# VectorE's 256 low-part columns of an attention block read from the score bank in PSUM, and one tile a block turned by TensorE in all four batches

## Chip, cores and metric

The kernel runs on one core of a Trainium2 chip. The metric is the device time of one execution in microseconds (us). Lower is better. The engines are TensorE (PE; its weight loads are listed apart, as PEld), VectorE (DVE), ScalarE (ACT), GpSimd (POOL) and SyncE (SP), which here only issues DMAs.

## What is computed

An attention with pooled keys, followed by a small MLP on 128 rows of each batch. The input has 4 batches of 12288 queries with 128 features; the keys and values of a batch are 768 rows, pooled 4 by 4 from 384 × 32 and projected by one matrix:

```python
kv_pool = kv.reshape(B, H // r, r, W // r, r, C).mean(axis=(2, 4))
k = v = kv_pool.reshape(B, -1, C) @ w_sr          # 768 x 128
s = scale * (q @ k.transpose(0, 2, 1))
s = s - s.max(-1, keepdims=True)
a = np.exp(s)
a /= a.sum(-1, keepdims=True) + 1e-09
x = (a @ v).astype(np.float32)
# then, per batch:
scores = np.einsum('bsd,d->bs', x, w_gate)
top_idx = np.argpartition(-scores[b], 128)[:128]
xe = x[b, top_idx]
ye = np.maximum(xe @ w1, 0.0) @ w2
out[b, top_idx] = xe + ye / (1.0 + np.exp(-scores[b, top_idx]))[:, None]
```

## The kernel before

A batch is cut into 48 blocks of 256 queries, 192 blocks in all, and one loop (L654) goes over them. A block is two groups (j = 0, 1) of 128 queries against 768 keys, so its scores are 128 partitions by 2 × 768 = 1536 columns of float32: exactly three PSUM banks of 512. There are two such buffers, s0 and s1, used in turn, and two banks for the outputs, o_two; together all eight banks of PSUM.

To keep float32 accuracy with 16-bit operands, numbers are split into a high part (float16) and a low part (bfloat16, the number minus its high part). That holds for the queries, the keys, the values and the exponentials. One iteration i works on several blocks at once:

- VectorE takes the row maximum of block i's scores (`s_max`, tile m).
- TensorE multiplies block i-4's exponentials with the values (`AV`, two groups of 18 matmuls, o_two<-vx,at).
- ScalarE takes the exponential of block i in three parts (`exp`): part 2 is bank 2 (columns 1024 to 1536), part 1 columns 768 to 1024, part 0 columns 0 to 768. It goes from the score buffer to the tile am in SBUF.
- TensorE computes the scores of block i+1 (`S`) in four pieces, 0: columns 0 to 512, 1: 512 to 768, 2: 768 to 1024, 3: 1024 to 1536. Each is three matmuls (kl, kb, kh). They overwrite the buffer of block i-1. Their order is 3, 2, 1, 0.
- The exponentials have to be turned (queries along the free axis, keys along the partitions) before `AV`. Eleven of the twelve 128-column tiles are turned by DMA: `to_high` casts them into hl's high part on ScalarE, `to_low` subtracts the high part, 1152 columns on GpSimd and 256 on VectorE, and `turn` issues one DMA transpose for the high and one for the low parts, from hl to at. The twelfth tile (columns from `CUT` = 1408) is turned by TensorE in batches 0 to 2 (`turn_pe`, a matmul with the identity, s<-cst,am, back into bank 2), then split by ScalarE and VectorE straight into at. In batch 3 `by_pe` is false, all twelve go by DMA, and VectorE subtracts 384 columns.
- VectorE normalises block i-4's output (`sums`, `recip`, `finish`; x<-o_two,rz), and SyncE writes it out every second block.

Beside this run the pooling and projection of the next batch's keys (`next_keys`, GpSimd additions and a few matmuls) and the search for the 128 largest scores of the batch before (`topk`), one step an iteration, at points that `at_point` names. They borrow room in the score buffer that is free (`borrow`).

Each engine runs its instructions in the order in which the code issues them (`InOrder`). A wait is put between engines where they touch the same bank or bytes; `declare_no_dep` takes away those that aren't needed. GpSimd's share of a block's subtraction is issued at the end of iteration i (L712), VectorE's share of it behind the maximum of iteration i+1 (L667).

Of the kernel before, what the change touches and what calls it, by code (L numbers as in the profile page):

```python
# [6 lines left out]
F32 = mybir.dt.float32  # L7
# [21 lines left out]
QT = 2  # L29
# [3 lines left out]
VC = C + 2  # L33
NCOL = N // P
CUT = 2 * M - P
SHARE = 1152
MID = 1.0 + 2.0 ** -8
FF = 1024
FT = FF // P
# [1 line left out]
class InOrder:  # L41
# [3 lines left out]
    seen = []  # L45
# [23 lines left out]
def attention_topk_mlp(ctx, tc, a, outs, capacity):  # L69
    nc = tc.nc  # L70
    pe, dve, act, pool = (InOrder(tc, e) for e in (nc.tensor, nc.vector, nc.scalar, nc.gpsimd))
# [22 lines left out]
    ident, tri, jrow, wg = (cst[:, i * P:(i + 1) * P] for i in range(4))  # L94
# [7 lines left out]
    s_flat = [x.rearrange("p k q -> p (k q)") for x in s_buf]  # L102
# [4 lines left out]
    room = {}  # L107

    def small_psum(shape, lo=0, side="select"):
        n = 1  # L110
        for x in shape[1:]:
            n *= x
        t = room[side][:, lo:lo + n]
        if len(shape) == 3:
            t = t.rearrange("p (a b) -> p a b", a=shape[1])
        return t

    def borrow(bank):
        room["prep"], room["select"], room["count"] = bank[:, 0:2 * P], bank[:, BANK:2 * BANK], bank[:, 2 * P:2 * P + 1]

    def load_kv(b, kc, parts=1, t=None):
        late = t is not None
# [225 lines left out]
    st = {}  # L348
# [14 lines left out]
    blocks = [(b, blk) for b in range(B) for blk in range(NBLK)]  # L363

    def S(n, parts=(0, 1, 2, 3), apart=(), only=(0, 1, 2)):
        b, blk = blocks[n]
        kh, kl, kb = (kvset[b][k] for k in ("kh", "kl", "kb"))
        qh, qt, ql = qsplit[b, blk]
        assert b == 0 or kvset[b].get("split") == KT
        for part in parts:  # L370
            lo, hi, j, k0 = ((0, 512, 0, 0), (512, 768, 0, 512), (768, 1024, 1, 0), (1024, 1536, 1, 256))[part]
            q = slice(j * P, (j + 1) * P)
            k = slice(k0, k0 + hi - lo)
            for i, (w, x) in enumerate(((qt, kl), (ql, kb), (qh, kh))):
# [11 lines left out]
    def by_pe(n):  # L386
        return blocks[n][0] < B - 1

    def exp(n, part):
        lo, hi, j = ((0, M, 0), (M, 2 * BANK, 1), (2 * BANK, 2 * M, 1))[part]  # L390
        if part == 2:
            st[n]["a"] = wk.tile([P, QT * M], F32, name="am")
            st[n]["hl"] = hlp.tile([P, 2, QT * M], U16, name="hl")
            st[n]["at"] = at.tile([P, 2, QT * KT, P], U16, name="at")
        r = act.activation(st[n]["a"][:, lo:hi], s_flat[n % 2][:, lo:hi], AF.Exp, bias=st[n]["m"][:, j:j + 1])
        st[n][f"exp{part}"] = r.ins
        for x in st[n].get("bank2", ()):
            tc.declare_no_dep(r.ins, x, reason="other banks")

    def turn_pe(n):  # L400
        r = pe.transpose(s_flat[n % 2][:, CUT:], st[n]["a"][:, CUT:], ident)
        tc.declare_no_dep(r.ins, st[n]["exp1"], reason="other banks")
        st[n].setdefault("bank2", []).append(r.ins)

    def halves(n, part):
        if part:
            a, hl = s_flat[n % 2][:, CUT:], [st[n]["at"][:, h, CUT // P:].rearrange("p t q -> p (t q)") for h in range(2)]
        else:
            hi = CUT if by_pe(n) else 2 * M
            a, hl = st[n]["a"][:, 0:hi], [st[n]["hl"][:, h, 0:hi] for h in range(2)]  # L410
        return a, hl[0].bitcast(F16), hl[1].bitcast(BF16)

    def to_high(n, part):
        st[n][part] = a, ah, al = halves(n, part)
        act.copy(ah, a)

    def to_low(n, part, engine, lo=0, hi=None):
        a, ah, al = (x[:, lo:hi] for x in st[n][part])
        r = engine.tensor_tensor(out=al, in0=a, in1=ah, op=ALU.subtract)
        if part:  # L420
            tc.declare_no_dep(r.ins, st[n]["exp0"], reason="other banks")

    def turn(n, h):
        k = CUT if by_pe(n) else 2 * M
        nc.sync.dma_start_transpose(out=st[n]["at"][:, h, 0:k // P], in_=st[n]["hl"][:, h, 0:k])

    def AV(n, j, dest=None):
        vx = kvset[blocks[n][0]]["vx"]
        assert kvset[blocks[n][0]].get("ready")
        ah, al = (st[n]["at"][:, h, j * KT:(j + 1) * KT].bitcast(t) for h, t in enumerate((F16, BF16)))  # L430
        if j == 0:
            st[n]["o"] = o_all if dest is None else dest
        o = st[n]["o"][:, j]
# [11 lines left out]
    def recip(n):  # L445
        dve.reciprocal(st[n]["rz"], st[n]["rz"])
# [182 lines left out]
    blocks = [(b, blk) for b in range(B) for blk in range(NBLK)]  # L629
# [24 lines left out]
    for i in range(nb):  # L654
        m = i - LAG + (i < TURN)
        old = m >= 0 and i != TURN
        b, blk = blocks[i]
        if blk % 2 == 0 and i + BPC < nb:
            nb_, nblk = blocks[i + BPC]
            load_q(nb_, nblk // BPC, nblk % BPC * BLK, (nblk % BPC + 2) * BLK)  # L660
        if blk == 0 and b + 1 < B:
            start(prep, next_keys(b + 1))
        if i:
            borrow(s_flat[(i - 1) % 2])
        s_max(i)
# [12 lines left out]
        InOrder.seen.clear()  # L678
        at_point("ev")
        bank1 = list(InOrder.seen)  # L680
        InOrder.seen.clear()
        at_point("up")
        at_point("t")
        at_point("cmp")
        at_point("g")
        more = 0 < i < nb - 1
        bank0 = list(InOrder.seen)
        if more:
            S(i + 1, (3,), bank0 + bank1)
        exp(i, 2)  # L690
        exp(i, 1)
        if by_pe(i):
            turn_pe(i)
            if more:
# [5 lines left out]
        if more:  # L700
            S(i + 1, (1,), bank0)
            S(i + 1, (0,))
        if old:
            sums(m)
            recip(m)
            finish(m)
        if by_pe(i):
            to_low(i, 1, dve)
        if i < nb - 1:
            to_high(i, 0)  # L710
            turn(i, 0)
            to_low(i, 0, pool, 0, SHARE)  # L712
        else:
            for lo, hi, copy in ((M, 2 * M, dve.tensor_copy), (0, M, act.copy)):
                x, h, l = (z[:, lo:hi] for z in halves(i, 0))
# [33 lines left out]
    high, low, eqh, rest = (tk.tile([P, NCOL], U16, name=x) for x in ("high", "low", "eqh", "rest16"))  # L749
# [93 lines left out]
```

## Time and profile before

| | |
|---|---|
| time, median of 3 runs | 1037.8 us (1035.89 to 1037.97) |
| profiled execution | 1037.92 us, span 1036.1 us |
| TensorE matmuls busy | 909.7 us, 88% |
| VectorE busy | 960.6 us, 93% |
| ScalarE busy | 743.9 us, 72% |
| GpSimd busy | 724.5 us, 70% |
| HBM read, written | 52.04 MB, 25.43 MB |

The span is the time from the first instruction's start to the last one's end in the profiled execution, and the time has 1.8 us more around it. Busy shares are averages over the span; matmuls are pipelined, so that their busy time isn't time at peak. In the views "a <- b" is output and inputs by their names in the program. L54 is the helper that records nearly all instructions, so groups are told apart by names and shapes.

### The profile page before, as it was taken

What the parts mean: (1) busy time and instruction counts of PE and PEld (TensorE: products, weight loads), DVE (VectorE), ACT (ScalarE), POOL (GpSimd) and SP (SyncE); (2) the same over time, 40 slices, a digit from 0 to 9 for tenths busy, and PEclk for the clock granted to TensorE, in tenths of its full rate; (3) what the DMA queues carried; (4) which work ended last, traced back from release to release, by engine and by line L of the source; (5) the groups of instructions that cost most, each with busy time, mean ns of one, the idle gap of its engine ahead of it and who ended that gap; (6) DMA issues with size and microseconds to landing.
All of it is one profiled execution on the core that took longest, in us unless ns stands there. A gap on an engine that the chain in (4) does not pass through costs nothing.

```text
span 1036.1 us, 26010 instructions
## 1 busy us (share of the span) xinstructions
PE 909.7 (88%) x9923; PEld 727.6 (70%) x9923; DVE 960.6 (93%) x2072; ACT 743.9 (72%) x1122; POOL 724.5 (70%) x487
## 2 busy tenths in 40 slices
PE   5799999989988999899978999889998899899854
PEld 4577777777777777777767777777776677677753
DVE  6899999999999999999889999999988999999975
ACT  2687778877977777778857777777877777778600
POOL 2588878877877877877767878778775666676500
PEclk9999999999999999999989999999999999999966
DMA  9899999999999999999989999999989999999920
GB/s 362 203 222 236 235 249 239 239 227 246 214 234 243 229 226 226 237 226 214 205 183 185 239 239 211 205 193 201 214 183 212 196 222 243 216 212 185 215 50 5
DMA packets 600509, 220.74 MB, mean 213 GB/s; under 512 B 569152, under 2 KB 570304, under 8 KB 599616
## 3 DMA queue, kind: packets, MB, share of 16 engines
q1 hardware_dynamic: 600128, 218.56, 100.7%
q8 instruction: 77, 1.26, 0.5%
q0 software_dynamic: 256, 0.52, 0.2%
q14 instruction: 48, 0.39, 0.1%
HBM read 52.04 MB, written 25.43 MB: 75 GB/s over the span
## 4 chain that ended last, share of the span: by engine, by line
DVE 31%; PE 23%; ACT 16%; issue 12%; DMA 11%; POOL 5%; SPq 1%; POOLq 0%; DVEq 0%; ACTq 0%
PE o_two L54 13%; DVE hl L54 11%; PE s L54 11%; DVE m L54 10%; DMA at<-hl 9%; ACT am L54 8%; ACT hl L54 8%; DVE junk L54 2%; DVE x L54 2%; POOL kv_sum L54 2%; DVE rz L54 2%; POOL hl L54 2%; DMA kv_raw<-in_kv 1%; POOL ql L54 1%; DVE sc L54 1%
## 5 line engine op out<-in xcount | busy, mean ns | idle before, releaser
L54 POOL TENSOR_TENSOR hl<-am,hl 128x1152 bf16<-128x1152 f32 x191 | 455.6, 2386 | 236.1 <-ACT hl L54 183.8
L54 PEld LDWEIGHTS <-at 128*128 128x128 f16 (+1 forms) x6912 | 410.5, 97 | 124.1 <-issue 112.2
L54 ACT ACTIVATE am<-s,m 128x512 f32<-128x512 f32 (+2 forms) x576 | 370.9, 687 | 167.5 <-DVE m L54 167.4
L54 PE MATMUL o_two<-vx,at 128*128 128x130 f16 x6804 | 431.4, 219 | 62.8 <-DVE x L54 52.3
L54 PE MATMUL s<-kh,qh 128*128 128x512 f32 (+1 forms) x768 | 362.8, 475 | 0.0
L54 DVE TENSOR_REDUCE m<-s 128x2 f32<-128x1536 f32 x192 | 336.1, 1751 | 20.0 <-PE s L54 19.3
L54 DVE TENSOR_TENSOR hl<-am,hl 128x256 bf16<-128x256 f32 (+2 forms) x193 | 327.9, 1700 | 0.5 <-ACT hl L54 0.5
L54 ACT CAST hl<-am 128x1408 f16<-128x1408 f32 (+1 forms) x192 | 266.7, 1389 | 6.1
L54 PE MATMUL s<-kl,qh 128*128 128x512 bf16 (+1 forms) x768 | 255.1, 332 | 9.6 <-DVE up L54 7.0
L54 PE MATMUL s<-kb,ql 128*128 128x512 bf16 (+1 forms) x768 | 250.9, 327 | 0.0
L54 PEld LDWEIGHTS s<-kh,qh 128*128 128x128 f32 x768 | 146.2, 190 | 50.5 <-issue 0.8
L54 POOL TENSOR_TENSOR ql<-q_raw,qh 128x512 bf16<-128x512 f32 x96 | 129.8, 1352 | 6.4 <-ACT qh L54 6.4
L54 PEld LDWEIGHTS <-qh 128*128 128x128 bf16 x768 | 77.8, 101 | 30.2 <-issue 12.9
L54 PEld LDWEIGHTS <-ql 128*128 128x128 bf16 x768 | 75.7, 99 | 15.1 <-issue 11.6
L54 DVE TENSOR_TENSOR x<-o_two,rz 128x256 f32<-128x256 f32 x189 | 78.4, 415 | 0.0
L54 POOL TENSOR_TENSOR kv_sum<-kv_raw 128x256 f32<-128x256 f32 x72 | 64.1, 891 | 0.0
L54 ACT CAST qh<-q_raw 128x512 fp32r<-128x512 f32 x96 | 58.9, 613 | 1.2 <-DMA q_raw<-in_q 1.2
L54 ACT CAST at<-s 128x128 f16<-128x128 f32 x144 | 38.3, 266 | 23.4 <-PE s L54 14.6
L54 PE MATMUL s<-cst,am 128*128 128x128 f32 x144 | 42.1, 292 | 14.5 <-ACT am L54 14.0
L54 PEld LDWEIGHTS s<-cst,am 128*128 128x128 f32 x144 | 20.1, 140 | 44.6 <-ACT am L54 43.3
L54 DVE TENSOR_TENSOR at<-s,at 128x128 bf16<-128x128 f32 x144 | 40.5, 281 | 2.9 <-ACT at L54 2.6
L54 DVE TENSOR_SCALAR rz<-o_two,sg 128x2 f32<-128x2 f32 x189 | 40.0, 212 | 1.5 <-PE o_two L54 1.4
(168 smaller groups left out, 533.5 us busy)
## 6 DMA issues: line engine op xcount, KB each, us to landing
out<-x SPq DMA_DIRECT2D x96, 256.0 KB, 3.4
q_raw<-in_q SPq DMA_DIRECT2D x93, 256.0 KB, 3.6
kv_raw<-in_kv SPq DMA_DIRECT2D x36, 512.0 KB, 4.8
kv_raw<-in_kv SPq DMA_DIRECT2D x6, 1024.0 KB, 7.4
at<-hl SPq DMA_TRANSPOSE x384, 3.9
w<-in_w SPq DMA_DIRECT2D x2, 512.0 KB, 9.5
q_raw<-in_q SPq DMA_DIRECT2D x1, 768.0 KB
cst<-in_cst SPq DMA_DIRECT2D x1, 320.0 KB
```

The costliest lines, as they stand in the source:

```text
L54: r = f(*args, **kwargs)
```

## The change

Part 1 of the exponential (columns 768 to 1024) is now written in place, into the score bank in PSUM, and no longer to am. ScalarE casts its 256 columns from there, and VectorE subtracts the high part from there; these 256 columns are VectorE's share (`OWN`). am has 1152 columns for GpSimd's share and 128 for the turned tile. The order of the tiles in hl and at changes with that (`ORDER` names the keys of each). TensorE's turned tile is now used in all four batches, and `by_pe` goes. In iterations that use the search's larger room in PSUM, that room is bank 2 only, and the score pieces come in the order 2, 1, 3, 0.

```diff
-SHARE = 1152
+OWN = 256
+SHARE = CUT - OWN
+ORDER = (2, 3, 4, 0, 1, 5)
...
         if part == 2:
-            st[n]["a"] = wk.tile([P, QT * M], F32, name="am")
-            st[n]["hl"] = hlp.tile([P, 2, QT * M], U16, name="hl")
+            st[n]["a"] = wk.tile([P, SHARE + P], F32, name="am")
+            st[n]["hl"] = hlp.tile([P, 2, CUT], U16, name="hl")
             st[n]["at"] = at.tile([P, 2, QT * KT, P], U16, name="at")
-        r = act.activation(st[n]["a"][:, lo:hi], s_flat[n % 2][:, lo:hi], AF.Exp, bias=st[n]["m"][:, j:j + 1])
+        x = s_flat[n % 2][:, lo:hi]
+        out = (st[n]["a"][:, 0:M], x, st[n]["a"][:, M:])[part]
+        r = act.activation(out, x, AF.Exp, bias=st[n]["m"][:, j:j + 1])
...
     def halves(n, part):
-        if part:
-            a, hl = s_flat[n % 2][:, CUT:], [st[n]["at"][:, h, CUT // P:].rearrange("p t q -> p (t q)") for h in range(2)]
+        if part == 0:
+            a, hl = st[n]["a"][:, 0:SHARE], [st[n]["hl"][:, h, 0:SHARE] for h in range(2)]
+        elif part == 1:
+            a, hl = s_flat[n % 2][:, M:2 * BANK], [st[n]["hl"][:, h, SHARE:] for h in range(2)]
         else:
-            hi = CUT if by_pe(n) else 2 * M
-            a, hl = st[n]["a"][:, 0:hi], [st[n]["hl"][:, h, 0:hi] for h in range(2)]
+            a, hl = s_flat[n % 2][:, CUT:], [st[n]["at"][:, h, CUT // P] for h in range(2)]
...
         s_max(i)
-        if i:
-            to_low(i - 1, 0, dve, SHARE)
-            turn(i - 1, 1)
         if old:
             AV(m, 0)
-            at_point("pe")
+        InOrder.seen.clear()
+        at_point("pe")
+        side = list(InOrder.seen)
+        if old:
             AV(m, 1)
         else:
-            at_point("pe")
             warm(18 if i == 0 else 24, banks[0][:, 0:P])
+        own = []
+        if i:
+            own = [to_low(i - 1, 1, dve)]
+            for y in side:
+                tc.declare_no_dep(own[0], y, reason="other banks")
+            turn(i - 1, 1)
...
+        order = (2, 1, 3, 0) if room["used"] else (3, 2, 1, 0)
+        clear = {0: own, 1: side, 2: side, 3: own if room["used"] else own + side}
...
+        score(0)
         exp(i, 2)
         exp(i, 1)
-        if by_pe(i):
-            turn_pe(i)
-            if more:
-                S(i + 1, (2,), bank0)
-            to_high(i, 1)
-        elif more:
-            S(i + 1, (2,), bank0)
+        turn_pe(i)
+        score(1)
+        to_high(i, 2)
         exp(i, 0)
...
-        if by_pe(i):
-            to_low(i, 1, dve)
+        to_low(i, 2, dve)
         if i < nb - 1:
+            to_high(i, 1)
             to_high(i, 0)
             turn(i, 0)
-            to_low(i, 0, pool, 0, SHARE)
+            to_low(i, 0, pool)
```

The first place is VectorE in a block of batch 1 with a search step; m is the row maximum, hl the split exponentials, s_107 and s_108 the two score buffers. Before:

```order
L54 TENSOR_TENSOR x<-o_two,rz 128x256
L54 TENSOR_TENSOR at<-s_108,at 128x128
L54 TENSOR_REDUCE m<-s_107 128x2
L54 TENSOR_TENSOR hl<-am,hl 128x256
L54 TENSOR_SCALAR up<-s_108 128x1
```

And now:

```order
L56 TENSOR_TENSOR x<-o_two,rz 128x256
L56 TENSOR_TENSOR at<-s_108,at 128x128
L56 TENSOR_REDUCE m<-s_107 128x2
L56 TENSOR_TENSOR hl<-s_108,hl 128x256
L56 TENSOR_SCALAR up<-s_108 128x1
```

Nothing has moved; the subtraction's first operand is the score buffer of the block before.

The second place is TensorE behind the score piece 3 of a block, where the turned tile (s_108<-cst,am) stands between the score pieces of the next block; a wait is named by the engine that is waited for. Before:

```order
L54 MATMUL s_107<-kh,qh 128x512
L54 MATMUL s_108<-cst,am 128x128 [waits Activation_49]
L54 LDWEIGHTS qh
L54 MATMUL s_107<-kl,qh 128x256
L54 LDWEIGHTS ql
L54 MATMUL s_107<-kb,ql 128x256
```

And now:

```order
L56 MATMUL s_107<-kh,qh 128x512
L56 MATMUL s_108<-cst,am 128x128 [waits Activation_49]
L56 LDWEIGHTS qh
L56 MATMUL s_107<-kl,qh 128x256 [waits DVE_49]
L56 LDWEIGHTS ql
L56 MATMUL s_107<-kb,ql 128x256
```

The order is the same, and the first matmul of piece 2 now waits for VectorE.

The third place is ScalarE in the last batch; am is the tile of exponentials in SBUF. Before:

```order
L54 ACTIVATE am<-s_107,m 128x512
L54 ACTIVATE am<-s_107,m 128x256
L54 ACTIVATE am<-s_107,m 128x768
L54 CAST hl<-am 128x1536
L54 ACTIVATE am<-s_108,m 128x512
```

And now:

```order
L56 ACTIVATE am<-s_108,m 128x512
L56 ACTIVATE s_108<-s_108,m 128x256
L56 CAST at<-s_108 128x128
L56 ACTIVATE am<-s_108,m 128x768
L56 CAST hl<-s_108 128x256
L56 CAST hl<-am 128x1152
```

The turned tile's cast has come in, the long cast is now two, and the second exponential stays in its bank. In the first three batches only the latter two are new.

## Rows read from the trace of the kernel before

**Rows 1.** The page: its first line, the busy time of each engine, and the data rate in 40 equal slices of the span.

```profile
span 1036.1 us, 26010 instructions
PE 909.7 (88%) x9923; PEld 727.6 (70%) x9923; DVE 960.6 (93%) x2072; ACT 743.9 (72%) x1122; POOL 724.5 (70%) x487
...
GB/s 362 203 222 236 235 249 239 239 227 246 214 234 243 229 226 226 237 226 214 205 183 185 239 239 211 205 193 201 214 183 212 196 222 243 216 212 185 215 50 5
```

**Rows 2.** Groups of instructions over the whole run, by form: line, engine, operation, names, shapes, count, then busy us and mean ns of one, then idle us before them.

```profile
L54 DVE TENSOR_REDUCE m<-s 128x2 f32<-128x1536 f32 x192 | 336.1, 1751 | 20.0 <-PE s L54 19.3 <-issue 0.2
L54 DVE TENSOR_TENSOR hl<-am,hl 128x256 bf16<-128x256 f32 x144 | 248.5, 1726 | 0.2 <-ACT hl L54 0.2
L54 ACT CAST hl<-am 128x1408 f16<-128x1408 f32 x144 | 196.7, 1366 | 4.6
...
L54 ACT ACTIVATE am<-s,m 128x256 f32<-128x256 f32 x192 | 89.8, 468 | 0.0
L54 DVE TENSOR_TENSOR x<-o_two,rz 128x256 f32<-128x256 f32 x189 | 78.4, 415 | 0.0
...
L54 DVE TENSOR_TENSOR hl<-am,hl 128x384 bf16<-128x384 f32 x47 | 77.6, 1652 | 0.3 <-ACT hl L54 0.3
...
L54 ACT CAST hl<-am 128x1536 f16<-128x1536 f32 x47 | 69.2, 1472 | 1.5
...
L54 DVE TENSOR_TENSOR at<-s,at 128x128 bf16<-128x128 f32 x144 | 40.5, 281 | 2.9 <-ACT at L54 2.6
...
L54 ACT CAST at<-s 128x128 f16<-128x128 f32 x144 | 38.3, 266 | 23.4 <-PE s L54 14.6
...
L54 ACT COPY kv_proj<-s 128x256 f32<-128x256 f32 x18 | 6.7, 373 | 13.5 <-PE s L54 13.4
```

**Rows 3.** Single tiles (hl, x and m): engine, operation, count, then the duration of one in ns (min/median/max), the first and last start in us, and shapes.

```profile
L54 DVE TENSOR_TENSOR hl<-am,hl x193: 409/1825/2404, 32.2 to 982.4; 128x256 bf16<-128x256 f32 x144, 128x384 bf16<-128x384 f32 x47, 128x768 bf16<-128x768 f32 x2
L54 DVE TENSOR_TENSOR x<-o_two,rz x189: 412/414/417, 48.1 to 984.0; 128x256 f32<-128x256 f32 x189
L54 DVE TENSOR_REDUCE m<-s x192: 1741/1748/1759, 26.5 to 976.4; 128x2 f32<-128x1536 f32 x192
```

**Rows 4.** One block of batch 0 in order of time: start in us, duration in us, engine, operation, names, shapes, count; in brackets the idle time of the engine ahead of it and what ended it.

```profile
126.16 1.75 DVE L54 TENSOR_REDUCE m<-s 128x2 f32<-128x1536 f32 x1
...
126.70 0.61 ACT L54 CAST qh<-q_raw 128x512 fp32r<-128x512 f32 x1
126.88 2.38 POOL L54 TENSOR_TENSOR hl<-am,hl 128x1152 bf16<-128x1152 f32 x1 [0.56 <-ACT hl L54]
...
127.83 1.71 DVE L54 TENSOR_TENSOR hl<-am,hl 128x256 bf16<-128x256 f32 x1
128.00 1.05 ACT L54 ACTIVATE am<-s,m 128x512 f32<-128x512 f32 x2 [0.69 <-DVE m L54]
...
128.74 0.14 PEld L54 LDWEIGHTS s<-cst,am 128*128 128x128 f32 x1 [0.18 <-ACT am L54]
128.82 0.27 PE L54 MATMUL s<-cst,am 128*128 128x128 f32 x1
...
128.93 0.27 PE L54 MATMUL s<-kl,qh 128*128 128x256 bf16 x1
...
129.28 0.28 PE L54 MATMUL s<-kl,qh 128*128 128x256 bf16 x1
...
129.63 0.39 PE L54 MATMUL s<-kl,qh 128*128 128x512 bf16 x1
...
129.89 0.58 PE L54 MATMUL s<-kh,qh 128*128 128x512 f32 x1
...
129.97 1.28 POOL L54 TENSOR_TENSOR ql<-q_raw,qh 128x512 bf16<-128x512 f32 x1
129.98 0.41 DVE L54 TENSOR_TENSOR x<-o_two,rz 128x256 f32<-128x256 f32 x1
130.24 1.37 ACT L54 CAST hl<-am 128x1408 f16<-128x1408 f32 x1
...
130.51 1.76 DVE L54 TENSOR_REDUCE m<-s 128x2 f32<-128x1536 f32 x1
```

**Rows 5.** The tile m by stages of the run: from and to in us, the length, busy us of VectorE (in brackets the number of row maxima, which is that of blocks) and of ScalarE's exponentials, the granted clock of TensorE as a share, the mean DMA share, GB/s. The stretch from 748 us on is that of batch 3; the last row is all from 614 us to the end of the loop.

```profile
66.00:262.00 196.00, 70.52 (x41) 79.71 (x122) 1.00 1.15 235
262.00:500.00 238.00, 83.55 (x48) 94.12 (x144) 1.00 1.11 228
500.00:614.00 114.00, 37.20 (x22) 41.17 (x63) 0.97 1.00 210
...
748.00:978.00 230.00, 83.84 (x48) 86.72 (x141) 0.99 1.06 211
...
614.00:978.00 364.00, 130.67 (x75) 139.67 (x222) 1.00 1.03 208
```

**Rows 6.** SyncE's DMA queue in order of time within the first of these stages (start, duration, queue, line, operation).

```profile
170.40 0.53 SPq L461 DMA_DIRECT2D out<-x  x1
171.03 3.62 SPq L425 DMA_TRANSPOSE at<-hl  x2
174.74 1.49 SPq L136 DMA_DIRECT2D q_raw<-in_q  x3
176.35 4.16 SPq L425 DMA_TRANSPOSE at<-hl  x2
```

**Rows 7.** Who waited for whom from 66 to 262 us: the two entries in which TensorE waits for a landed transpose (us in total, times, longest).

```profile
PEld L54 <- DMA at<-hl: 9.8, 16, 1.5
PE o_two L54 <- DMA at<-hl: 5.7, 12, 1.3
```

**Rows 8.** Who waited for whom from 500 to 614 us (the first two rows) and from 614 to 978 us (the last): us in total, times, longest.

```profile
ACT am L54 <- DVE m L54: 21.7, 16, 6.5
...
PEld s L54 <- ACT am L54: 10.1, 16, 5.9
...
ACT am L54 <- DVE m L54: 72.8, 65, 5.6
```

**Rows 9.** A block's maximum and the two transposes issued for it, in order of time; then, from the DMA issues between 262 and 500 us, the transposes with their count and the median us from issue to landing.

```profile
400.74 1.75 DVE L54 TENSOR_REDUCE m<-s 128x2 f32<-128x1536 f32 x1
...
408.21 4.28 SPq L425 DMA_TRANSPOSE at<-hl  x2
...
at<-hl SPq DMA_TRANSPOSE x98, 4.0
```

More of the change, by code (lines that the diff above doesn't have):

```diff
@@ L106, in attention_topk_mlp @@
     banks = [o_two[:, j] for j in range(QT)]
-    room = {}
+    room = {"used": False}
     def small_psum(shape, lo=0, side="select"):
         n = 1
+        room["used"] |= side == "select"
         for x in shape[1:]:
@@ L118, in borrow @@
     def borrow(bank):
-        room["prep"], room["select"], room["count"] = bank[:, 0:2 * P], bank[:, BANK:2 * BANK], bank[:, 2 * P:2 * P + 1]
+        room["prep"], room["select"], room["count"] = bank[:, 0:2 * P], bank[:, 2 * BANK:], bank[:, 2 * P:2 * P + 1]
+        room["used"] = False
     def load_kv(b, kc, parts=1, t=None):
@@ L384, in s_max @@
         st[n] = {"m": m}
-    def by_pe(n):
-        return blocks[n][0] < B - 1
     def exp(n, part):
@@ L391, in exp, with others @@
         if part == 2:
-            st[n]["a"] = wk.tile([P, QT * M], F32, name="am")
-            st[n]["hl"] = hlp.tile([P, 2, QT * M], U16, name="hl")
+            st[n]["a"] = wk.tile([P, SHARE + P], F32, name="am")
+            st[n]["hl"] = hlp.tile([P, 2, CUT], U16, name="hl")
             st[n]["at"] = at.tile([P, 2, QT * KT, P], U16, name="at")
-        r = act.activation(st[n]["a"][:, lo:hi], s_flat[n % 2][:, lo:hi], AF.Exp, bias=st[n]["m"][:, j:j + 1])
+        x = s_flat[n % 2][:, lo:hi]
+        out = (st[n]["a"][:, 0:M], x, st[n]["a"][:, M:])[part]
+        r = act.activation(out, x, AF.Exp, bias=st[n]["m"][:, j:j + 1])
         st[n][f"exp{part}"] = r.ins
-        for x in st[n].get("bank2", ()):
+        if part < 2:
+            others(r, st[n].get("bank2", ()))
+    def others(r, seen):
+        for x in seen:
             tc.declare_no_dep(r.ins, x, reason="other banks")
     def turn_pe(n):
-        r = pe.transpose(s_flat[n % 2][:, CUT:], st[n]["a"][:, CUT:], ident)
-        tc.declare_no_dep(r.ins, st[n]["exp1"], reason="other banks")
-        st[n].setdefault("bank2", []).append(r.ins)
+        r = pe.transpose(s_flat[n % 2][:, CUT:], st[n]["a"][:, SHARE:], ident)
+        others(r, [st[n]["exp1"]])
+        st[n]["bank2"] = [r.ins]
     def halves(n, part):
-        if part:
-            a, hl = s_flat[n % 2][:, CUT:], [st[n]["at"][:, h, CUT // P:].rearrange("p t q -> p (t q)") for h in range(2)]
-        else:
-            hi = CUT if by_pe(n) else 2 * M
-            a, hl = st[n]["a"][:, 0:hi], [st[n]["hl"][:, h, 0:hi] for h in range(2)]
+        if part == 0:
+            a, hl = st[n]["a"][:, 0:SHARE], [st[n]["hl"][:, h, 0:SHARE] for h in range(2)]
+        elif part == 1:
+            a, hl = s_flat[n % 2][:, M:2 * BANK], [st[n]["hl"][:, h, SHARE:] for h in range(2)]
+        else:
+            a, hl = s_flat[n % 2][:, CUT:], [st[n]["at"][:, h, CUT // P] for h in range(2)]
         return a, hl[0].bitcast(F16), hl[1].bitcast(BF16)
@@ L414, in to_high, with to_low @@
         st[n][part] = a, ah, al = halves(n, part)
-        act.copy(ah, a)
-    def to_low(n, part, engine, lo=0, hi=None):
-        a, ah, al = (x[:, lo:hi] for x in st[n][part])
+        r = act.copy(ah, a)
+        if part == 1:
+            others(r, st[n]["bank2"] + [st[n]["low2"]])
+        elif part == 2:
+            others(r, [st[n]["exp1"]])
+            st[n]["bank2"].append(r.ins)
+    def to_low(n, part, engine):
+        a, ah, al = st[n][part]
         r = engine.tensor_tensor(out=al, in0=a, in1=ah, op=ALU.subtract)
-        if part:
-            tc.declare_no_dep(r.ins, st[n]["exp0"], reason="other banks")
+        st[n][f"low{part}"] = r.ins
+        if part == 2:
+            others(r, [st[n]["exp0"], st[n]["exp1"]])
+        return r.ins
     def turn(n, h):
-        k = CUT if by_pe(n) else 2 * M
-        nc.sync.dma_start_transpose(out=st[n]["at"][:, h, 0:k // P], in_=st[n]["hl"][:, h, 0:k])
+        nc.sync.dma_start_transpose(out=st[n]["at"][:, h, 0:CUT // P], in_=st[n]["hl"][:, h])
     def AV(n, j, dest=None):
@@ L435, in AV @@
         for i, (w, h, kt) in enumerate(mm):
-            pe.matmul(o, w[:, kt], vx[:, h, kt], start=(i == 0), stop=(i == len(mm) - 1))
+            pe.matmul(o, w[:, kt], vx[:, h, ORDER[kt] if j else kt], start=(i == 0), stop=(i == len(mm) - 1))
     def sums(n):
@@ L678, in attention_topk_mlp, with score @@
         InOrder.seen.clear()
[L679 to L685, printed above, removed]
-        more = 0 < i < nb - 1
-        bank0 = list(InOrder.seen)
-        if more:
-            S(i + 1, (3,), bank0 + bank1)
+        for point in ("ev", "up", "t", "cmp", "g"):
+            at_point(point)
+        side = list(InOrder.seen)
+        for x in side:
+            for y in own:
+                tc.declare_no_dep(x, y, reason="other banks")
+        more = 0 < i < nb - 1
+        order = (2, 1, 3, 0) if room["used"] else (3, 2, 1, 0)
+        clear = {0: own, 1: side, 2: side, 3: own if room["used"] else own + side}
+        def score(k):
+            if more:
+                S(i + 1, (order[k],), clear[order[k]])
+        score(0)
         exp(i, 2)
         exp(i, 1)
-        if by_pe(i):
-            turn_pe(i)
-            if more:
-                S(i + 1, (2,), bank0)
-            to_high(i, 1)
-        elif more:
-            S(i + 1, (2,), bank0)
+        turn_pe(i)
+        score(1)
+        to_high(i, 2)
         exp(i, 0)
-        if more:
-            S(i + 1, (1,), bank0)
-            S(i + 1, (0,))
+        score(2)
+        score(3)
         if old:
@@ L706, in attention_topk_mlp @@
             finish(m)
-        if by_pe(i):
-            to_low(i, 1, dve)
+        to_low(i, 2, dve)
         if i < nb - 1:
+            to_high(i, 1)
             to_high(i, 0)
             turn(i, 0)
-            to_low(i, 0, pool, 0, SHARE)
+            to_low(i, 0, pool)
         else:
-            for lo, hi, copy in ((M, 2 * M, dve.tensor_copy), (0, M, act.copy)):
-                x, h, l = (z[:, lo:hi] for z in halves(i, 0))
+            for part, copy in ((1, dve.tensor_copy), (0, act.copy)):
+                x, h, l = halves(i, part)
                 copy(h, x)
```

## Prediction

> **What bounds the kernel now.** I read the page's busy table first, then the groups of instructions by form, then single tiles, then one block in order of time, and last the stages of the run with their DMA traffic.
>
> The page says that VectorE is busy 93% of the span, more than any other engine [rows 1]. The groups show how it is spent: 1751 ns a block on the row maximum, and 1726 ns on a subtraction of only 256 columns (1652 ns for 384 columns in the last batch) [rows 2]. That second figure isn't work. The normalisation of 256 columns, also a two-input VectorE operation, takes 412 to 417 ns in all its 189 instances, while the subtraction runs from 409 to 2404 ns with a median of 1825 [rows 3]. The block in order of time shows what it waits for: GpSimd's own subtraction runs from 126.88 to 129.26 us, VectorE's starts at 127.83 and ends at 129.54, 0.28 us behind GpSimd's end [rows 4]. So VectorE holds an issued instruction until GpSimd is through, then does it. Both its tensor inputs are in SBUF. At 129.98 the same block has the counter-example: the normalisation, one tensor input from PSUM and one from SBUF, starts 0.01 us into a GpSimd operation of 1.28 us and still takes 0.41 us [rows 4].
>
> Two other limits stand close behind. The first is a chain that needs no VectorE beyond the maximum. In rows 4 the maximum starts at 126.16; the exponential starts at 128.00, the turned tile's weight load at 128.74 and its matmul at 128.82; the remaining three score pieces follow at 128.93, 129.28 and 129.63, the last product ends at 130.47, and the next maximum starts at 130.51: 4.35 us. The second is the DMA queue. From 66 to 262 us there are 41 maxima in 196 us, 4.78 us a block, at 235 GB/s and a DMA share of 1.15 [rows 5]; SyncE's queue issues back to back there, each row beginning where the last one ended, to 0.11 us [rows 6]; and TensorE waits for landed transposes, 9.8 and 5.7 us, only there: the whole run's sums are the same two [rows 7]. This stage is limited by DMA already, not by VectorE. From 262 on nothing waits for a transpose, and the rate falls to 228, 210 and 208 GB/s at 4.96, 5.18 and 4.85 us a block [rows 5].
>
> **The change, part by part.** *The low part from PSUM.* In the first three batches VectorE's order stays the same; only the first operand of the 256-column subtraction moves from am to the score bank. Its price is not in the trace as such. The nearest row is the 256-column normalisation with one PSUM and one SBUF input, 415 ns; the 128-column subtraction of the turned tile, the same operation from PSUM, takes 281 [rows 2, 3]. Below: nothing under 281. Above: 1726, should it still be held. I take 415, since the nearest row has the same size and operand kinds and passes GpSimd. VectorE loses 144 × 1.31 + 47 × 1.24 = 247 us of its 960.6 busy us and gains 48 × 0.28 = 13 for the turned tile of the last batch: 727 us, 3.8 us a block at most. It stops being the bound.
>
> *A wait on TensorE.* The score piece behind the turned tile now waits for VectorE, as its order shows, since the low part reads the bank that this piece overwrites. VectorE reads right behind its maximum: maximum's end 127.91 + 0.42 = 128.33, while the piece isn't reached before 128.93 [rows 4]. Cost nothing, with 0.6 us to spare; without that cover every block's chain grows by what is lacking. Behind the piece stand two more pieces and the next maximum.
>
> *ScalarE.* The 1408-column cast becomes one of 256 columns from PSUM and one of 1152. A 256-column copy from PSUM takes 373 ns; 1152 columns, from 1366 at 1408 and 1472 at 1536 (0.83 ns a column), 1154 ns: 0.16 us more a block [rows 2]. The exponential of 256 columns writes PSUM in place; the nearest row is its 468 ns into SBUF, and I take that; 0.2 us either way doesn't matter, because ScalarE stood idle 0.69 us before its exponentials in rows 4, even with a cast of 0.61 us in between. That idle time hides both; without it they lengthen the chain. The exponential ahead of the turned tile is not touched.
>
> *The last batch.* All 48 blocks now turn a tile on TensorE: 0.11 us there (128.82 to 128.93), a cast of 266 ns, and a subtraction of 281 ns, against 128 columns less of everything that goes to the DMA queue. But the score pieces now stand behind the exponential, so that this batch too gets the chain of 4.35 us, where it ran at 4.8 (48 blocks in 230 us [rows 5]).
>
> **The sum.** What a stage becomes is the larger of two limits: the chain, for which I take 4.43 us (4.35 and an allowance of 0.08 for blocks with projections and key casts), and DMA at 235 GB/s, the rate of the stage that it limits.
> - 0 to 66 us, loading and the first blocks: unchanged.
> - 66 to 262: at the DMA limit; unchanged, 196.
> - 262 to 500: 228 × 238 = 54.3 MB; at 235 GB/s 231 us, 4.81 a block. 7 less.
> - 500 to 614: 210 × 114 = 23.9 MB would need 102 us. The chain gives 22 × 4.43 + 8 = 106; the 8 are for two long blocks, with waits of 6.5 and 5.9 us [rows 8], which the change doesn't touch. 8 less.
> - 614 to 978: 75 blocks [rows 5], 75 × 4.43 + 7 = 339 (7 again for long blocks, wait 5.6 [rows 8]); DMA, 208 × 364 = 75.7 MB, would need 322. 25 less.
> - 978 to the end: unchanged, 58.
> - A head start: at 262 the transposes lead. A block with its maximum at 400.74 issues its two transposes from 408.21 to 412.49 and they land 4.0 us after issue, the second by some 414.6 [rows 9]; its values are wanted four blocks on, 400.74 + 4 × 4.96 = 420.6. TensorE can eat these 6 us before DMA limits it: I take 5.
>
> 66 + 196 + 231 + 106 + 339 + 58 − 5 = 991 us of span, against 1036.1. The profiled execution took 1037.92, 1.8 above its span and equal to the median of 1037.8 within 0.1. So **993 us**. On VectorE 247 us go and some 45 come back as time; the stall moves to TensorE's wait for transposes up to some 600 us, and behind that to VectorE's wait for the scores.
>
> **Rivals.**
> *DMA isn't at its limit.* The page's slices reach 249 GB/s [rows 1], so 235 could be what was asked for. But rows 6 and 7 speak for a limit. If there is none, 66 to 262 becomes 41 × 4.43 = 182, and 262 to 614 70 × 4.43 + 8 = 318 in place of 332: 14 and 14 more, or 965 us. The Trainium skill (DMA: Bandwidth & Descriptors, Latency and other measured facts) gives 261 GB/s for transposes on one kernel. At that rate a block's 1.12 MB would take 4.3 us, and DMA would never bind; the 235 of a stage in which TensorE waits for transposes speaks against it.
> *DMA limits more.* If the rate of 228 GB/s from 262 to 500 is already all that this mix allows, and ScalarE's extra cast costs half of the last stage's gain, only 8 + 12 remain: 1018 us.
> *No change.* The critical stall moves to DMA everywhere: 1036 us.
> *Slower: the read is held all the same.* Should VectorE's subtraction still wait for GpSimd, TensorE's new wait puts GpSimd into the chain. From a maximum it is 1.84 us to the exponential (126.16 to 128.00), 3.61 to the end of the cast (131.61), 2.38 for GpSimd, 0.28, then 1.54 for three score pieces (128.93 to 130.47) and 0.04 to the maximum of two blocks on: 9.69, or 4.85 a block; another GpSimd subtraction of 1.28 (row 129.97) ahead of it in every second block makes 5.5. At their mean, 5.2 against today's 4.97 (maxima from 26.5 to 976.4, 191 steps [rows 3]), that is 191 × 0.23 = 44 more: 1082 us. It decides from a subtraction of about 1.0 us up (0.42 and the 0.6 to spare). The Trainium skill (PSUM — Partial Sum Buffer, PSUM bank collisions raise a hardware error) says that two engines must not use one bank at once and that the chip doesn't stall to prevent it; by that the wait is needed, whatever it costs. Against this rival stand the 189 normalisations with no instance above 417 ns.
>
> **How the numbers follow.** About 993 (978 to 1008): 0.50. No DMA limit (955 to 978): 0.21. DMA or ScalarE limiting more (1008 to 1035): 0.20. No change: 0.03. Slower: 0.06. The range 962 to 1021 leaves out about 2 in 10: the rivals' outer ends, no change and slower. A measurement of this kernel can tell about 0.2% from no change. Faster 0.91, same 0.03, slower 0.06.
>
> **What the profile after would show.** VectorE's subtraction of 256 columns near 415 ns with hardly any spread; VectorE's busy share near 73%; a TensorE wait for landed transposes of tens of us where it was 15.5, spread to 600 us; blocks of 4.3 to 4.5 us behind 614; the row maximum waiting for TensorE. Wrong would be: subtractions above 1 us (held after all), a rate well above 235 GB/s between 66 and 500 (no DMA limit), or ScalarE without idle time before its exponentials.

## The result, and the profile after

The changed kernel takes 985.36 us (median of 4 runs, 981.34 to 988.03) against 1037.74: a ratio of 0.9496 (0.9456 to 0.9535). Its profiled execution took 987.41 us, 1.8 above its span.

The first lines of the page after, and its data rates in 40 slices, to be held against [rows 1]:

```profile
span 985.6 us, 26392 instructions
...
PE 902.0 (92%) x9971; PEld 717.7 (73%) x9971; DVE 754.2 (77%) x2120; ACT 748.2 (76%) x1361; POOL 691.4 (70%) x487
...
GB/s 360 222 232 213 237 257 229 251 236 249 231 215 221 246 245 232 234 236 218 238 221 214 228 220 242 245 231 237 212 174 227 226 232 241 214 213 209 198 39 7
```

VectorE falls from 93% to 77%, and TensorE is now the busiest engine. The groups by form, with the columns of [rows 2]:

```profile
L56 DVE TENSOR_REDUCE m<-s 128x2 f32<-128x1536 f32 x192 | 337.4, 1757 | 112.9 <-PE s L56 112.4
L56 ACT CAST hl<-am 128x1152 f16<-128x1152 f32 x192 | 225.3, 1173 | 0.0
...
L56 ACT ACTIVATE s<-s,m 128x256 f32<-128x256 f32 x192 | 86.0, 448 | 6.3
L56 DVE TENSOR_TENSOR hl<-s,hl 128x256 bf16<-128x256 f32 x192 | 79.6, 415 | 0.1
...
L56 ACT CAST hl<-s 128x256 f16<-128x256 f32 x191 | 71.2, 373 | 0.0
```

The subtraction takes 415 ns where it took 1726, and the row maximum, which hardly waited before, waits 112.4 us for TensorE's scores. The tile hl (columns as in [rows 3]) shows that no instance is held any more:

```profile
L56 DVE TENSOR_TENSOR hl<-s,hl x192: 405/415/425, 32.0 to 932.4; 128x256 bf16<-128x256 f32 x192
```

One block of batch 3 in order of time, to be read beside [rows 4]:

```profile
748.15 1.76 DVE L56 TENSOR_REDUCE m<-s 128x2 f32<-128x1536 f32 x1 [0.78 <-PE s L56]
749.24 2.38 POOL L56 TENSOR_TENSOR hl<-am,hl 128x1152 bf16<-128x1152 f32 x1 [1.36 <-PE s L56]
749.82 0.41 DVE L56 TENSOR_TENSOR hl<-s,hl 128x256 bf16<-128x256 f32 x1
750.00 0.69 ACT L56 ACTIVATE am<-s,m 128x512 f32<-128x512 f32 x1 [0.32 <-DVE m L56]
...
750.74 0.14 PEld L56 LDWEIGHTS s<-cst,am 128*128 128x128 f32 x1 [0.28 <-ACT am L56]
...
750.91 0.27 PE L56 MATMUL s<-kl,qh 128*128 128x256 bf16 x1
...
751.86 0.58 PE L56 MATMUL s<-kh,qh 128*128 128x512 f32 x1
...
752.48 1.76 DVE L56 TENSOR_REDUCE m<-s 128x2 f32<-128x1536 f32 x1 [0.51 <-PE s L56]
```

VectorE's subtraction starts 0.58 us into a GpSimd operation of 2.38 us and is done in 0.41. It ends at 750.23, 0.68 us before the score piece that must wait for it (750.91). The block is 4.33 us long, and its end is set by the chain: maximum, first exponential, turned tile, three score pieces, next maximum.

Stages, for the tile m, with the columns of [rows 5]:

```profile
66.00:262.00 196.00, 71.27 (x41) 82.92 (x123) 0.98 1.15 239
262.00:500.00 238.00, 86.09 (x49) 100.52 (x148) 0.99 1.15 232
500.00:600.00 100.00, 35.16 (x20) 41.32 (x61) 0.98 1.14 224
600.00:930.00 330.00, 130.01 (x74) 149.34 (x220) 1.00 1.12 221
```

From 66 to 262 us there are 41 blocks, as before. TensorE's waits for landed transposes (total us, times, longest) were all in the first stage before [rows 7]. After, over the whole run, then from 490 to 600 us, then from 600 to 930:

```profile
PEld L56 <- DMA at<-hl: 45.8, 48, 5.2
PE o_two L56 <- DMA at<-hl: 32.7, 31, 5.1
...
PEld L56 <- DMA at<-hl: 9.2, 6, 5.2
PE o_two L56 <- DMA at<-hl: 7.7, 4, 5.1
...
PEld L56 <- DMA at<-hl: 0.8, 2, 0.5
PE o_two L56 <- DMA at<-hl: 0.2, 1, 0.2
```

The two entries of a pair must not be added: a weight load and its matmul wait for the same landing, and taken together their waits cover 46.0 us after and 9.8 before, hardly more than the weight loads' alone. The prediction's 15.5 is such a sum. So the stall moved to the transposes up to 600 us; behind that it is TensorE's chain. The starts of the row maxima tell where the 50.5 us of span came from:

| start of maximum number | before, us | after, us | gained since the row above |
|---|---|---|---|
| 49 | 261.58 | 258.42 | 3.2 |
| 97 | 500.54 | 490.23 | 7.2 |
| 119 | 619.06 | 600.25 | 8.5 |
| 192 (last) | 976.45 | 927.87 | 29.8 |
| end of span | 1036.14 | 985.64 | 1.9 |

### The profile page after: what moved, and what is told of

Its sections match the earlier page's. It is cut to its first block, busy times and chain, and to the rows that moved or that the text cites. A ratio compares the mean times of both kernels' runs of the same rounds, so it can differ in the third digit from the quotient of the medians.

```text
span 985.6 us, 26392 instructions
## 1 busy us (share of the span) xinstructions
PE 902.0 (92%) x9971; PEld 717.7 (73%) x9971; DVE 754.2 (77%) x2120; ACT 748.2 (76%) x1361; POOL 691.4 (70%) x487
## 4 chain that ended last, share of the span: by engine, by line
PE 54%; DMA 15%; DVE 9%; issue 8%; ACT 7%; POOL 6%; SPq 0%; POOLq 0%; DVEq 0%; ACTq 0%
PE s L56 30%; PE o_two L56 25%; DMA at<-hl 13%; ACT am L56 4%; DVE m L56 3%; POOL hl L56 3%; ACT hl L56 2%; POOL kv_sum L56 2%; DMA kv_raw<-in_kv 1%; DVE junk L56 1%; POOL ql L56 1%; ACT s L56 1%; DVE pooled L56 0%; DVE hl L56 0%; DVE mg L56 0%
## 5 line engine op out<-in xcount | busy, mean ns | idle before, releaser
L56 PEld LDWEIGHTS <-at 128*128 128x128 f16 (+1 forms) x6912 | 400.1, 97 | 90.6 <-DMA at<-hl 45.8
L56 DVE TENSOR_REDUCE m<-s 128x2 f32<-128x1536 f32 x192 | 337.4, 1757 | 112.9 <-PE s L56 112.4
L56 ACT ACTIVATE am<-s,m 128x512 f32<-128x512 f32 (+1 forms) x384 | 306.1, 797 | 100.4 <-DVE m L56 99.5
L56 ACT CAST hl<-am 128x1152 f16<-128x1152 f32 x192 | 225.3, 1173 | 0.0
L56 POOL TENSOR_TENSOR ql<-q_raw,qh 128x512 bf16<-128x512 f32 x96 | 122.7, 1278 | 6.7 <-ACT qh L56 6.7
L56 ACT ACTIVATE s<-s,m 128x256 f32<-128x256 f32 x192 | 86.0, 448 | 6.3
L56 DVE TENSOR_TENSOR hl<-s,hl 128x256 bf16<-128x256 f32 x192 | 79.6, 415 | 0.1
L56 ACT CAST at<-s 128x128 f16<-128x128 f32 x192 | 50.9, 265 | 34.2 <-PE s L56 33.8
L56 DVE TENSOR_TENSOR at<-s,at 128x128 bf16<-128x128 f32 x192 | 55.0, 286 | 21.9 <-ACT at L56 18.3
L56 ACT CAST hl<-s 128x256 f16<-128x256 f32 x191 | 71.2, 373 | 0.0
L56 PE MATMUL s<-cst,am 128*128 128x128 f32 x192 | 61.1, 318 | 8.1 <-ACT am L56 7.7
```

The source lines that it names most:

```text
L56: r = f(*args, **kwargs)
```

## The experiments

The theory: the subtraction was held because both inputs were in SBUF while GpSimd worked; read from PSUM it is free, and DMA transposes then limit up to 600 us, the chain through the turned tile behind. The rivals: the gain comes from the turned tile of the last batch, or from the new cut of ScalarE's work; DMA isn't the limit. Each ratio is against the kernel before, run on the same chip.

### Undo the PSUM read alone

Everything of the change stays, but the 256 columns go to am in SBUF again.

```diff
-            st[n]["a"] = wk.tile([P, SHARE + P], F32, name="am")
+            st[n]["a"] = wk.tile([P, SHARE + P + OWN], F32, name="am")
-        out = (st[n]["a"][:, 0:M], x, st[n]["a"][:, M:])[part]
+        out = (st[n]["a"][:, 0:M], st[n]["a"][:, SHARE + P:], st[n]["a"][:, M:SHARE + P])[part]
-            a, hl = s_flat[n % 2][:, M:2 * BANK], ...
+            a, hl = st[n]["a"][:, SHARE + P:], ...
```

> The changed kernel with one thing undone: the second exponential goes to am in SBUF again, and VectorE's 256 columns and their cast are read from there. Order, split casts and the turned tile in all batches stay. Theory (VectorE is held while GpSimd reads SBUF, if both its inputs are in SBUF): its 256-column subtraction is back at a mean of 1300 to 1800 ns, each overlapping one ending 0.28 us behind GpSimd's, and the time at 1025 to 1042 us. Rival (the gain comes from the other edits: the cast in two, the turned tile in the last batch, the place of the subtraction): below 1000 us.

Measured: 1041.8 us, ratio 1.0049 (1.003 to 1.0069). VectorE is at 93% again. The tile hl in this kernel:

```profile
L56 DVE TENSOR_TENSOR hl<-am,hl x193: 408/1761/2398, 31.9 to 981.3; 128x256 bf16<-128x256 f32 x192, 128x1152 bf16<-128x1152 f32 x1
```

Same size, same order, same neighbours; only where the 256 columns lie differs (with ScalarE's write and cast of them), and the median goes from 415 to 1761 ns and the time up by 56 us. All instances of the traces say what the one in [rows 4] says. Here 188 of the 193 subtractions start while a GpSimd operation runs, and every one of these ends 0.28 to 0.38 us behind that operation's end; in the kernel before it is 186 of 193, and 0.28 to 0.42 us. Those of 256 columns that start with GpSimd idle take 0.41 to 0.43 us in both. In the changed kernel 190 of 192 start beside a GpSimd operation and none takes more than 0.43. The Trainium skill (SBUF — State Buffer, SBUF: two separate sides) says that VectorE and GpSimd share a pair of SBUF ports as an exclusive lock: whichever starts first holds it for the whole instruction, GpSimd with any operation, VectorE with one that runs in a two-port mode or that has two SBUF inputs, the latter only against a GpSimd operation that reads SBUF. This case agrees: VectorE ends behind GpSimd in all these instances, and these two kernels show that one input in PSUM suffices to escape it.

### The turned tile of the last batch alone, on the kernel before

```diff
     def by_pe(n):
-        return blocks[n][0] < B - 1
+        return n < len(blocks) - 1
```

> The kernel before with the other part alone: one tile turned by TensorE in the last batch too (all but its last block); VectorE's columns stay in SBUF, 256 of them in all batches. Theory: VectorE is held in the last batch as before, and gets a subtraction of 0.28 us more there, so nothing of the last batch's 19 us comes: 1033 to 1043 us. Rival (the last batch gains because fewer tiles go by DMA): about 1019 us.

Measured: 1048.06 us, ratio 1.0108 (1.0091 to 1.0125): slower, and 5 us above the expected range. The tile m from 750 to 978 us, in the kernel before and then in this one:

```profile
750.00:978.00 228.00, 82.09 (x47) 86.72 (x141) 0.99 1.05 210
...
750.00:978.00 228.00, 79.80 (x46) 88.12 (x135) 0.99 0.94 189
```

One block fewer fits into the stretch although the DMA rate falls from 210 to 189 GB/s: this fits VectorE still being the bound, with one instruction more a block. This half of the change, by itself, costs time.

### The PSUM read alone

The changed kernel, with the twelve tiles of batch 3 turned by DMA as before and GpSimd subtracting 1280 columns there.

```diff
+FULL = 2 * M - OWN
+    def by_pe(n):
+        return blocks[n][0] < B - 1
-            a, hl = st[n]["a"][:, 0:SHARE], ...
+            k = SHARE if by_pe(n) else FULL
+            a, hl = st[n]["a"][:, 0:k], ...
-        turn_pe(i)
+        if by_pe(i):
+            turn_pe(i)
```

> The changed kernel with the other part undone: in the last batch all twelve tiles go by DMA again (GpSimd subtracts 1280 columns there, VectorE its 256 from PSUM). Theory (VectorE's read from PSUM is the gain; the turned tile only swaps the chain of 4.33 us for a DMA limit in the last batch): there the chain is gone, and DMA has 0.79 MB of transposes and 0.26 MB besides a block, 4.46 us at 235 GB/s: 2 to 8 us more than the changed kernel, 984 to 996 us. Rival (the turned tile brings the last batch's gain of 19 us): 1000 us or more.

Measured: 987.63 us, ratio 0.9509 (0.9467 to 0.955). The interval overlaps that of the whole change (0.9456 to 0.9535), so the read from PSUM is the gain, and the turned tile adds nothing that these runs can tell. Its waits, of the same two kinds:

```profile
PEld L57 <- DMA at<-hl: 53.0, 59, 5.0
...
PE o_two L57 <- DMA at<-hl: 37.4, 43, 4.8
```

The weight loads wait 53.0 us in place of 45.8. In batch 3 a block without the turned tile repeats every 4.15 us where nothing holds it, but four behind 760 us take 5.0 to 6.4, with waits for transposes of 0.9 to 2.5 us in them: a shorter chain is paid back in waits for DMA.

### Half of the transposes left out, after and before

Both leave out the transposes of the low parts and multiply the high part twice, so that their outputs are not the reference's.

```diff
-        ah, al = (st[n]["at"][:, h, j * KT:(j + 1) * KT].bitcast(t) for h, t in enumerate((F16, BF16)))
+        ah, al = (st[n]["at"][:, 0, j * KT:(j + 1) * KT].bitcast(t) for t in (F16, BF16))
-            turn(i - 1, 1)
-            turn(i, 1)
```

> The changed kernel without the DMA transposes of the low parts; the values' matmuls for the low parts read the high parts' tiles instead, so TensorE does the same work, and the output is not the reference's. Theory (behind 66 us the DMA rate of about 235 GB/s is the limit up to some 680 us, and behind that the chain of 4.33 us a block): no wait for landed transposes, nearly all blocks of the first three batches at 4.33 us, 935 to 955 us. Rival (the long blocks of the first three batches come from ScalarE's and GpSimd's work for the next keys, not from DMA): 975 to 990 us.

> The kernel before without the DMA transposes of the low parts, in the same way (the output is not the reference's). Theory (VectorE, held behind GpSimd, limits all but the stage from 66 to 262 us): few us less, 1015 to 1037. Rival (DMA limited the kernel before all along, and VectorE's 93% were only in its shade): about 40 us less, below 1000.

Measured: the changed kernel goes to 943.19 us, ratio 0.9099 (0.908 to 0.9119); the kernel before to 1032.15, ratio 0.9951 (0.9934 to 0.9969). These transposes cost the changed kernel 42 us and the old one 5. In the first, no wait for a transpose is left, and the median block is 4.33 us in every batch; the tile m in its first three stages:

```profile
66.00:262.00 196.00, 78.01 (x45) 90.30 (x133) 1.00 0.73 166
262.00:500.00 238.00, 91.61 (x53) 107.87 (x159) 1.00 0.80 173
500.00:600.00 100.00, 40.16 (x23) 45.76 (x68) 1.00 0.71 163
```

45, 53 and 23 blocks in place of 41, 49 and 20. In the second, VectorE's subtraction is held as ever:

```profile
L54 DVE TENSOR_TENSOR hl<-am,hl x193: 409/1821/2516, 32.5 to 975.8; 128x256 bf16<-128x256 f32 x144, 128x384 bf16<-128x384 f32 x47, 128x768 bf16<-128x768 f32 x2
```

Between these two kernels the change is worth 89 us, against 52 with all transposes: 37 of the gain go to the transposes. The rival "DMA isn't at its limit" falls. But before, these transposes cost only 5 us: the stage with the same 41 blocks was near two limits at once.

### The turned tile one score piece later

```diff
-        turn_pe(i)
         score(1)
+        turn_pe(i)
```

> The changed kernel with TensorE's turned tile one score piece later (piece 2 ahead of it, pieces 1 and 0 behind it). Theory (a block of 4.33 us is the chain maximum, exponential, turned tile, the pieces behind it, next maximum; DMA limits the stage up to some 600 us): the chain loses a piece of 0.345 us, TensorE's own work of 4.2 us becomes the limit of the blocks that DMA leaves free; those behind 600 us gain 0.1 us each, 974 to 982 us in all. Rival (TensorE's own work is the 4.33): 983 to 988.

Measured: 975.86 us, ratio 0.9426 (0.9396 to 0.9457), 9.5 us less than the changed kernel; the two intervals just touch, but all four runs of this one are below all four of that. TensorE's wait for the exponential that the tile needs, in the changed kernel and then in this one:

```profile
PEld s L56 <- ACT am L56: 51.3, 144, 3.5
...
PEld s L56 <- ACT am L56: 6.9, 15, 2.9
```

The blocks behind 600 us have a median of 4.24 in place of 4.33 us. So the chain through the exponential is what bounded there.

The same edit on the kernel without low-part transposes (whose outputs are again not the reference's) shows what TensorE alone allows.

> The changed kernel without the low parts' transposes (output not the reference's) and with the turned tile one piece later: with DMA out of the way, this measures what is behind the chain. Theory: all blocks at TensorE's own 4.2 us, 192 x 0.1 us less than the 943 us with the turned tile in its old place: 918 to 932 us. Rival (4.33 us is TensorE's own work): 940 to 946.

Measured: 934.34 us, ratio 0.9004 (0.8985 to 0.9023), 9 us less than without the edit, 2 above what was expected. The median block is 4.22 to 4.27 us in every stage, not 4.2, and blocks with other work are longer: the size was off, the place right.

### Two tiles turned by TensorE, one fewer by DMA

```diff
-CUT = 2 * M - P
+CUT = 2 * M - 2 * P
-ORDER = (2, 3, 4, 0, 1, 5)
+ORDER = (2, 3, 0, 1, 4, 5)
+        for k in range(2):
             r = pe.transpose(s_flat[n % 2][:, CUT + k * P:CUT + (k + 1) * P], ...
```

> The changed kernel with two tiles a block turned by TensorE and ten by DMA. DMA theory: a block's 1.12 MB becomes 1.06, so the 110 blocks up to some 600 us, 4.87 us each, become 4.59: 31 us less; the chain gets a second transpose of 0.11 us, 8 us more behind 600 us: 955 to 970 us. Rival (TensorE and ScalarE have no room for it, or the number of transposes counts and not their size): 983 or more.

> Both at once: two tiles by TensorE, one score piece later. Theory: 31 us less up to 600 us, and behind it TensorE's own 4.2 + 0.11 us, as in the changed kernel: 946 to 960 us. Rival (as for two tiles alone): 983 or more.

Measured: 976.07 us, ratio 0.942 (0.9398 to 0.9442), and with the tiles one piece later 971.09, ratio 0.9379 (0.9351 to 0.9408): better than the changed kernel, both short of what was expected. The waits for transposes in the first of them are nearly gone:

```profile
PEld s L56 <- ACT am L56: 60.1, 163, 4.0
...
PEld L56 <- DMA at<-hl: 3.2, 7, 1.4
PE o_two L56 <- DMA at<-hl: 1.8, 3, 1.2
```

but its chain is longer, 4.44 us a block in all batches. As many transposes are issued as before, each smaller: that their number counts and not their size, the rival, doesn't fit. Up to maximum 119 this kernel gains 28 us (572.3 against 600.2), and from there to the last maximum it loses 12 (339.9 against 327.6). 31 and 8 had been reckoned. The second tile costs 0.11 us on TensorE in each block, whether DMA limits there or not, which makes 8 of the 12; block 149, 8.17 us long, adds 3.7, with a step of the search, VectorE's key<-sc, beside GpSimd:

```profile
717.38 4.15 DVE L56 TENSOR_SCALAR key<-sc 128x96 int32<-128x96 int32 x1
...
719.30 2.14 POOL L56 TENSOR_TENSOR hl<-am,hl 128x1024 bf16<-128x1024 f32 x1
```

It ends 0.09 us behind GpSimd's operation, and takes 0.20 us in the changed kernel's batch 3. So a VectorE operation with a single SBUF input is held as well, and the change removed the hold of one group only. In the second kernel, blocks are 4.35 us, and key<-key,sc of the same step takes 4.02.

### Two tiles where DMA limits, one behind

```diff
+FEW = 118
+    def tiles(n):
+        return 2 if n < FEW else 1
+    def cut(n):
+        return 2 * M - tiles(n) * P
-        turn_pe(i)
         score(1)
+        turn_pe(i)
```

> Two turned tiles in blocks 0 to 117, where DMA limits the changed kernel, one in the rest, and the turned tiles one score piece later throughout. Theory (DMA limits to block 118, TensorE's own work behind it): as with two tiles and the later turn up to block 118 (576.8 us in its profile), and as with one tile and the later turn behind it (326 us from there to the last maximum, where two tiles took 333): 958 to 970 us. Rival (the later turn's gains belong to runs of few us of difference and do not add): 971 or more.

Measured: 961.18 us, ratio 0.9266 (0.9237 to 0.9294), 24 us less than the changed kernel and the best that was run. Its page and its waits:

```profile
PE 892.3 (93%) x9903; PEld 722.9 (75%) x10089; DVE 769.5 (80%) x2120; ACT 753.4 (78%) x1361; POOL 663.3 (69%) x487
```

```profile
PEld L54 <- DMA at<-hl: 20.0, 27, 2.0
...
PE o_two L54 <- DMA at<-hl: 13.1, 21, 1.8
```

Maximum 119 starts at 578.1 (600.2 in the changed kernel), and the blocks behind it are at 4.24 us.

## Why the prediction was right, point by point

**The read from PSUM: right.** 415 ns was taken from the normalisation, and 415 is the mean of 192 instances between 405 and 425. The row with the same size and the same kinds of operands gave the price; undoing the read alone shows that the place of the input is the cause. The rival "held all the same" falls with it.

**Cost nothing for the new wait: right.** 0.68 us to spare in the block shown, 0.6 reckoned; TensorE's waits for this read are 0.3 us in the whole run.

**ScalarE: right in the main.** 373 ns for the cast from PSUM as taken, 1173 for 1154, 448 in place for 468; it stays off the path but for its first exponential, which was in the chain that the forecast used.

**Up to 262 us: right, with a reading that goes too far.** Nothing was expected, and 3.2 us came. That is no gain that can be told from chance: the kernel before with the turned tile in the last batch alone runs the same instructions up to batch 3, and its maximum 49 starts at 258.58 us, 3.0 ahead of the kernel before. The first stage was limited by transposes, as [rows 5 to 7] said, but "not by VectorE" goes too far: taking half of them from the kernel before brought only 5 us, since VectorE stood right behind.

**262 to 500 us: right.** 7 were expected and 7.2 came, at 232 GB/s and 4.83 us a block on average (4.81 forecast). The limit isn't spread evenly: the median block is 4.33 us, and a few of 6 to 9 us carry the waits.

**500 to 614 us: right in size, in part by luck.** 8 were expected, 8.5 came. The forecast let the chain set this stage, with 8 us for two long blocks "which the change doesn't touch". Neither holds. TensorE waits for transposes there, 9.2 us from 490 to 600, and without the low parts' transposes the 22 blocks from maximum 97 to 119 take 100.3 us in place of 110.0. And the waits of 6.5 and 5.9 us in [rows 8] are those of ScalarE and TensorE in one and the same block, whose maximum came late since VectorE's search step key<-key,sc was held too. The kernel before, with the GpSimd operation that ends just ahead of it, then the same step in the changed kernel:

```profile
527.29 5.49 DVE L54 TENSOR_TENSOR key<-key,sc 128x96 int32<-128x96 int32 x1
...
531.38 1.26 POOL L54 TENSOR_TENSOR kv_sum<-kv_sum 128x512 f32<-128x512 f32 x1
...
515.17 0.67 DVE L56 TENSOR_TENSOR key<-key,sc 128x96 int32<-128x96 int32 x1
```

Block 101 goes from 10.06 to 4.33 us with it. That gain was not in the forecast, and waits for transposes took as much away.

**The head start: not shown.** The forecast counted 5 us for transposes that lead at 262. No such term appears. What makes up its size in the sum is the 3.2 us up to 262, no more than chance as said, and 1.9 behind the last maximum; here the sum was lucky.

**614 to 978 us: right mechanism, size off by 5.** 25 less was expected, 29.8 came. The term has two errors of about the same size. The 73 steps from maximum 119 to the last took 357.4 us before and 327.6 after, so 4.90 and 4.49 each; the forecast's 364 and 339 us over 75 blocks are 4.85 and 4.52. The allowance of 0.08 for blocks with other work wasn't needed in most: the median is 4.327 us, and the long blocks make the difference to 4.49. They aren't the one that the forecast's 7 us were taken from: block 149, 8.94 us before with key<-sc held for 3.88, takes 4.33 after. Others are long, 145 to 147 with 5.33, 5.29 and 6.06 above all; that 7 and the allowance fit them is chance.

**VectorE's busy time: too low.** 727 us was expected, 754 came. By the groups the subtraction lost 246 us, as worked out, and the turned tile gained 14.5 in place of 13; but the page's busy time fell by only 206. Of the other 26, 20 are overlap: the records of neighbouring VectorE instructions overlap by 108.5 us in all before and 88.1 after, and the page counts such time once. The rest lies in small groups.

**The turned tile of the last batch: an open point in the forecast, settled.** The forecast put it into the gain of the last stage without parting the two. On the kernel before it costs 10 us; with the PSUM read it makes no difference that these runs can tell: the chain that it lengthens and the DMA work that it saves come to about the same there.

## What to carry to other kernels

When the same operation has two durations in one profile, look at where its inputs lie and what GpSimd does meanwhile: moving one input to PSUM, where the result stood anyway, took 1.3 us off VectorE's subtraction in every block. Look at small operations too: search steps of 0.2 to 0.3 us took up to 5.5 when GpSimd was at work. Then ask which limit stands next, stage by stage: here 37 of the 89 us that the change gives with half of the transposes gone went to waits for them, and it paid to share work differently in the stages with different limits (two turned tiles where DMA limits, one behind). The order of two neighbours on the engine in the chain (a turned tile one score piece later) brought another 9 us for no work at all.

## What was not expected of the hardware

A wait for a transpose can cost more than itself. In the changed kernel eleven blocks between 66 and 600 us are 6 to 11 us long, ten of them with such a wait. In the one shown here TensorE waits for a transpose until 135.61 (columns as in [rows 4]):

```profile
130.89 0.58 PE L56 MATMUL s<-kh,qh 128*128 128x512 f32 x1
...
135.61 0.35 PEld L56 LDWEIGHTS <-at 128*128 128x128 bf16 x6 [2.03 <-DMA at<-hl]
...
138.43 0.99 PE L56 MATMUL s<-kh,qh 128*128 128x512 f32 x1
```

The same matmul takes 0.58 us before the wait and 0.99 behind it. The stretches before, right behind, and after that (busy us of PE, PEld, DVE, ACT, POOL with counts, then TensorE's granted clock, DMA share, GB/s):

```profile
131.00:135.60 4.60, 2.76 (x25) 1.79 (x23) 3.10 (x7) 3.59 (x7) 3.03 (x3) 1.00 1.24 221
135.60:137.80 2.20, 2.19 (x27) 2.18 (x28) 0.30 (x2) 1.09 (x3) 2.20 (x3) 0.82 1.15 259
137.80:141.00 3.20, 3.20 (x17) 2.20 (x14) 1.17 (x5) 1.64 (x5) 0.66 (x1) 0.59 0.96 267
```

The granted clock goes from 1.00 (2.4 GHz) to a mean of 0.59, mostly the lower level of 1.2 GHz, after TensorE had been busy 2.76 of 4.60 us. An estimate from these rows: 2.2 × 0.18 + 3.2 × 0.41 = 1.7 us of work lost, nearly as much as the wait of 2.03. This isn't so in every long block. Over the whole of this block, and over one of those in which the clock stayed:

```profile
133.10:141.47 8.37, 6.51 (x57) 5.07 (x55) 3.55 (x9) 4.73 (x9) 4.28 (x3) 0.80 1.13 240
...
464.11:471.57 7.46, 5.35 (x63) 4.32 (x64) 3.51 (x11) 3.47 (x9) 2.36 (x1) 1.00 1.04 240
```

Four of the ten are at 0.79 to 0.84, and six at 1.00, the second one shown with two waits of up to 2.5 us among them. In the kernel without low-part transposes none of the ten is left, and the clock is 1.00 up to 600 us; the eleventh, block 99 with 6.05 us of its own work on TensorE, stays. That the low clock follows from the wait, and not from something else that goes with it, was not tried by itself, and what parts the four from the six stays open.
